# Four shared 8 KB tiles for early heads and first weights, in a clustered attention, FFN and soft-MoE kernel

## The chip, the cores and the metric

The kernel runs on one core of one Trainium2 chip. The metric is device time in microseconds (us) of one execution, lower is better. A core has five engines, each with its own instruction queue that runs in order: PE (TensorE, matrix products), DVE (VectorE), ACT (ScalarE), POOL (GpSimd) and SP (SyncE, which here only issues DMAs). An engine that comes to an instruction whose inputs are not ready waits, and everything behind it in its queue waits too.

## The reference

Three stages follow one another. In the first, 16 pairs of batch and head (2 x 8, called heads below) each have 768 tokens of 64 numbers; every query and key is put to its nearest of 16 centroids, and attention is restricted to pairs of the same cluster. The second is a feed-forward layer, and the third a soft mixture of 8 experts with 4 slots each, whose slot weights are a softmax over all 1,536 tokens and whose combine weights are a softmax over the 32 slots:

```python
q_assign = np.argmax(np.einsum('bhsd,hcd->bhsc', q_n, c_n), axis=-1)
scores = np.where(mask, scale * np.matmul(q, k.transpose(0, 1, 3, 2)), -1000000000.0)
x = softmax(scores) @ v                      # [1536, 512] after merging heads
h = x @ w_in                                 # [1536, 2048]
x = (h * np.clip(h + 3.0, 0.0, 6.0) / 6.0) @ w_out
logits = x @ phi                             # [1536, 32]
slot_input = softmax(logits, axis=0).T @ x   # [32, 512]
slot_out[e] = np.maximum(slot_input[e] @ w1[e], 0.0) @ w2[e]
out = softmax(logits, axis=1) @ slot_out     # [1536, 512]
```

## The kernel before, in words

Everything is one core's work; large products are done on fp16 pairs (a high part and the remainder). The 1,536 tokens are 12 tiles of 128, six to a batch.

**Stages.** Attention (up to about 300 us) goes head by head. For head i: `load` fetches q, k and v; `cast_hi` and `cast_lo` split q and k; a transposing DMA on SP turns them into `qk1t_i`; `as_mm` and `as_max` find each token's cluster; `as_put` writes the cluster marks beside q and k, and a second transposing DMA makes `qk2t_i`; `maxq` (products into the tile sm_i_n, L534) and `maxr` (a DVE reduction into mxs, L550) find the row maxima for the six tiles; `shift` (L557, L559) turns the maxima with PE and writes them into rows 96 to 101 of qk2t_i with DVE; only then can `scores` (L572, L576, tiles st_i_t) begin, followed by `exps`, `plow` and `pv`. Beside the heads run the preparation of the FFN weights (`win`, `wout`, `narrow` with lines L893, L895 and L897, which turns 64-bit weights into 32-bit ones) and, for tiles of the first batch, the token stage: `hid` (L726, tile h), `act` (tiles r and ghl, turned into gt either by a DMA or, for tiles 6, 7, 10 and 11, by PE into the tile gp and a copy, L763 and L768), `logits` (lg, L777), column maxima, and the slot sums `dispatch` (z, L834). The second batch's tokens follow from 300 to about 390 us. Then come slot inputs (zt, si, sit), expert layer 1 (e, L1393), layer 2 (o, L1430 and L1450), the slot outputs (so, L1336) and the combination (po, L1370) with the output DMAs.

**What sets the order.** Each function is a generator, one piece of work per `yield`, entered once as an event with `ev`. `flush` runs the pieces in the order of a long string of event numbers, ORDER. A second string, ROOMS, names for most tiles which of a tag's buffers they take. Filler products (`keep`, tile kw, L363) compute nothing that is used; there are 136 of them.

**Weights of the experts.** 36 chunks of 1 MB (four of them the product of w_out and phi's side, `wos`; sixteen of w1; sixteen of w2) are fetched by `fetch` (L1019 to L1076) into rooms: 4 in ring_a, 10 in ring_b, 1 in ring_c and others in tiles that the token stage gives up (x, w0 to w3, r, ghl, gt). Ring_b's rooms exist only once the pool of the attention tiles is closed (`close`, L1160). The last ten chunks reuse rooms that layer 1 has read:

```python
rooms = ["a"] * NRA + ["b"] * NRB + ["c"] * NRC + ["x.g", "w0", "w1", "w2", "w3", "x.r", "ghl", "gt", "ghl"]
rooms += ["a"] * 2 + ["b"] * 9 + ["c"]
```

**The end.** `slots_out(p)` and `combine(p, b)` (L1351 to L1386) run for p = 0 (384 of the 512 output columns) and p = 1 (128), and for each batch b. For p = 0 a batch has three pairs of tiles, copied out of PSUM by ACT and DVE in turn; the first two pairs share one output DMA of 768 KB (L1381), the third has one of 384 KB (L1384). Batch 0's DMAs are issued by ACT, batch 1's by SP.

Of the kernel before, what the change touches and what calls it, by code (L numbers as in the profile page):

```python
# [222 lines left out]
NRA = 4  # L223
WHOLE = ("024", "024", "024", "024", "024", "024", "024", "024", "", "", "", "", "", "", "", "")
TURNED = {6, 7, 10, 11}
NRB = 10
NRC = 1


@with_exitstack  # L230
def clustered_attention_ffn_softmoe(ctx: ExitStack, tc, q, k, v, cent, w_in, w_out, phi, w1, w2, out):
# [924 lines left out]
    for n in range(NRA):  # L1156
        evf()
# [368 lines left out]
```

## Time and profile before

| | us |
|---|---|
| median of 3 runs | 454.58 |
| the three runs | 454.5, 454.58, 462.92 |
| the profiled execution, its own time | 454.56 |
| its span, first to last instruction or DMA | 452.6 |
| mean granted clock of PE over the span | 0.989 of full |

The profile is one execution. Its times count from the span's start. The time of an execution is the span and some 2 us around it.

### The profile page before, as it was taken

Reading aid. Unit: us, or ns where it says so; the run is one execution under the profiler, and the core shown is the slowest. Engines: PE = TensorE matmul, PEld = TensorE weight load, DVE = VectorE, ACT = ScalarE, POOL = GpSimd, SP = SyncE. Lnnn points to the kernel's source line nnn. Section 1 sums busy time; section 2 is a strip of 40 time slices with the busy share of each in tenths; the row PEclk is TensorE's granted clock in tenths of the full one; section 3 lists DMA queues with packets and bytes.
Section 4 is the critical chain, followed back from the end, with each engine's and each line's share of the span. In section 5 each row is a group of like instructions: output and inputs, shape, how many; then the busy total and the mean of one; then the engine's idle time right before and its main releaser. Section 6 shows DMA issues by size and latency. Waiting matters only on the chain.

```text
span 452.6 us, 11711 instructions
## 1 busy us (share of the span) xinstructions
PE 430.9 (95%) x4866; PEld 275.6 (61%) x4866; DVE 275.5 (61%) x481; ACT 307.3 (68%) x506; POOL 251.8 (56%) x229
## 2 busy tenths in 40 slices
PE   7899999999999989999999999999999999789982
PEld 6567877787887555666656567764655455523332
DVE  5999988999877587465736768512543236621223
ACT  7799997999999868978887897974343545301011
POOL 6558695775756675797876777994133323130000
PEclk9999998999999999999999999999999999989998
DMA  7999766977596996367831876009999999999978
GB/s 268 267 240 244 185 144 197 222 215 217 211 285 105 307 191 135 111 136 138 156 100 37 276 138 94 4 2 222 240 337 313 310 232 290 326 314 353 383 195 279
DMA packets 126612, 95.23 MB, mean 210 GB/s; under 512 B 95328, under 2 KB 111712, under 8 KB 126560
## 3 DMA queue, kind: packets, MB, share of 16 engines
q1 hardware_dynamic: 122656, 88.69, 75.1%
q10 hardware_dynamic: 3904, 5.80, 3.5%
q8 instruction: 38, 0.62, 0.6%
q14 instruction: 14, 0.11, 0.1%
HBM read 64.06 MB, written 7.34 MB: 158 GB/s over the span
## 4 chain that ended last, share of the span: by engine, by line
PE 80%; DMA 7%; DVE 6%; ACT 3%; POOL 1%; issue 1%; SPq 0%; ACTq 0%; DVEq 0%
PE h L726 26%; PE acc L642 7%; PE st L572 6%; PE st L576 6%; PE sm L534 6%; DMA wk<-in_moe_w_dram 5%; PE acc L648 3%; PE acc L647 3%; PE acc L655 3%; PE z L834 2%; PE kw L363 2%; PE lg L777 2%; PE tp L966 1%; DMA qk1t<-qk 1%; DVE mxs L550 1%; PE gp L763 1%
## 5 line engine op out<-in xcount | busy, mean ns | idle before, releaser
L354 POOL TENSOR_TENSOR pp<-p,pp 128x768 f16<-128x768 f32 x72 | 119.1, 1661 | 52.4 <-ACT pp L344 25.2
L726 PE MATMUL h<-wq,xt 128*128 128x512 f16 x576 | 134.4, 379 | 0.0
L550 DVE TENSOR_REDUCE mxs<-sm 128x1 f32<-128x768 f32 x96 | 89.6, 953 | 22.9 <-PE sm L534 21.8
L726 PEld LDWEIGHTS <-xt 128*128 128x128 f16 x576 | 54.1, 97 | 58.2 <-issue 1.7
L354 POOL TENSOR_TENSOR ghl<-r,ghl 128x1024 f16<-128x1024 f32 (+1 forms) x25 | 50.3, 2015 | 56.8 <-ACT ghl L344 56.7
L620 ACT ACTIVATE p<-st 128x768 f32<-128x768 f32 x72 | 57.7, 808 | 10.8 <-PE st L576 9.2
L344 ACT ACTIVATE pp<-p 128x768 f16<-128x768 f32 x72 | 60.4, 844 | 1.7 <-PE acc L655 0.7
L572 PE MATMUL st<-qk1t 128*128 128x384 f16 x192 | 47.2, 327 | 1.4 <-DVE qk2t L559 1.2
L576 PE MATMUL st<-qk2t 102*128 102x384 f16 x192 | 47.3, 327 | 0.0
L534 PE MATMUL sm<-qk2t 80*128 80x384 f16 x192 | 45.2, 325 | 1.5 <-DVE wi L897 0.8
L743 ACT ACTIVATE r<-h,b_relu 128x1024 f32<-128x1024 f32 (+1 forms) x26 | 27.0, 1049 | 25.8 <-PE h L726 12.3
L745 DVE SCALAR_TENSOR_TENSOR r<-r,h 128x1024 f32<-128x1024 f32 (+1 forms) x26 | 29.4, 1136 | 19.5 <-ACT r L743 19.3
L344 ACT ACTIVATE ghl<-r 128x1024 f16<-128x1024 f32 (+1 forms) x26 | 25.5, 988 | 17.3 <-DVE r L745 10.6
L648 PE MATMUL acc<-v,pp 128*128 128x64 f16 x432 | 36.4, 194 | 0.0
L647 PE MATMUL acc<-v,pp 128*128 128x65 f16 x432 | 36.4, 193 | 0.0
L642 PE MATMUL acc<-v,pp 128*128 128x65 f32 x288 | 35.8, 274 | 0.3 <-DVE ohs L477 0.2
L642 PEld LDWEIGHTS acc<-v,pp 128*128 128x128 f32 x288 | 34.8, 192 | 1.9 <-DVE ohs L477 0.6
L647 PEld LDWEIGHTS <-pp 128*128 128x128 f16 x432 | 31.6, 100 | 4.0 <-issue 0.8
L354 POOL TENSOR_TENSOR qk<-qk,qk 128x768 f16<-128x768 f32 x15 | 24.7, 1646 | 12.1 <-ACT qk L344 11.1
L648 PEld LDWEIGHTS <-pp 128*128 128x128 f16 x432 | 29.5, 96 | 3.1
L344 ACT ACTIVATE qk<-qk 128x768 f32<-128x768 f32 (+2 forms) x32 | 26.3, 822 | 3.7 <-DMA qk1t<-qk 2.6
L576 PEld LDWEIGHTS <-qk2t 102*128 102x128 f16 x192 | 18.8, 98 | 13.1 <-issue 0.7
(197 smaller groups left out, 763.0 us busy)
## 6 DMA issues: line engine op xcount, KB each, us to landing
wk<-in_moe_w_dram SPq DMA_DIRECT2D x48, 512.0 KB, 5.9
wi<-in_moe_w_in_dram SPq DMA_DIRECT2D x16, 512.0 KB, 5.8
wod<-in_moe_w_out_dram SPq DMA_DIRECT2D x16, 512.0 KB, 5.3
wos<-wo ACTq DMA_DIRECT2D x8, 512.0 KB, 3.1
wk<-wos SPq DMA_DIRECT2D x8, 512.0 KB, 6.9
qk<-in_q_dram SPq DMA_DIRECT2D x16, 192.0 KB, 3.4
qk<-in_k_dram SPq DMA_DIRECT2D x16, 192.0 KB, 5.0
v<-in_v_dram SPq DMA_DIRECT2D x16, 192.0 KB, 2.9
```

The costliest lines, as they stand in the source:

```text
L344: nc.scalar.activation(out, in_, AF.Copy, scale=scale)
L354: (nc.vector if e == "v" else nc.gpsimd).tensor_tensor(out=out, in0=in_, in1=hi, op=ALU.subtract)
L534: nc.tensor.matmul(s[:, j, 0:384], d["qk2t"][0:80, n, 0], d["qk2t"][0:80, 3 * j : 3 * j + 3, 1], start=True, stop=True,)
L550: nc.vector.tensor_reduce(out=mxs[i % 2][:, 96 + n : 97 + n], in_=s[:, :, 0:384], op=ALU.max, axis=AX.XY)
L572: nc.tensor.matmul(s[:, j, 0:384], d["qk1t"][:, t, 1], d["qk1t"][:, 3 * j : 3 * j + 3, 0], start=True, stop=False)
L576: nc.tensor.matmul(s[:, j, 0:384], d["qk2t"][0 : 96 + NT, t, 1], d["qk2t"][0 : 96 + NT, 3 * j : 3 * j + 3, 0], start=False, stop=True,)
L620: nc.scalar.activation(p32, s[:, :, 0:384], AF.Exp, scale=sc_exp)
L642: nc.tensor.matmul(o, p32[:, j, r * P : (r + 1) * P], d["v32"][:, t], start=(t == 0 and n == 0), stop=False)
L647: nc.tensor.matmul(o, hi, v1[:, t, 0:65], start=(t == 0 and n == 0), stop=False)
L648: nc.tensor.matmul(o[:, 0:64], hi, v1[:, t, 65:129], start=False, stop=False)
L726: nc.tensor.matmul(s[:, fb % 2], xt[:, lhs], wq[fb][:, hl, kk], start=(n == 0), stop=(n == 11))
L745: nc.vector.scalar_tensor_tensor(out=g, in0=r, scalar=6.0 * SG, in1=sf, op0=ALU.min, op1=ALU.mult)
```

## The change

Four tiles `pr_0` to `pr_3` of 8 KB per partition are made once, beside the constants, and live through the whole kernel. `piece` cuts smaller tiles out of them. During attention they hold the two q/k load tiles and the staging copy `sp` (pr_0); the split q/k tile, the centroid tiles and narrow's scratch (pr_1); two of the three qk2 tiles, v of the even heads and the centroid pair (pr_2); qk1t and qk2t of heads 0, 4, 8 and 12 and v of the odd heads (pr_3). So v has two buffers in place of one, qk1t and qk2t have three and a shared one in place of four, and ring_b shrinks from 10 rooms to 6. The four tiles then take weight chunks 4 to 7, which no longer have to wait for the attention pool to close, and later chunks 26 to 29.

Chunk 16 goes into two tiles of turned activations (x.x) in place of x.r, and late_x moves to the tag r. The last token tile's copies of gt, all four on DVE before, go half to ACT. For p = 0 `combine` issues one DMA of 384 KB per pair of tiles. In layer 1 the events stay, and the new ORDER runs expert group 0's first two steps, group 1's first three, then group 0's last two and group 1's last. Numbering of events changes (HEADS, the interleaving of win and wout), and ORDER and ROOMS are new throughout. PE has as many instructions as before, 136 fillers included.

```diff
-    "9 0 8 12 15 0 9 16 12 12 817 15 16 1 807 7 10 835 8 838 11 816 16 16 16 16 8 825 834 8 836 4 16 8 17 20 13 0 "
...
+    "0 837 807 9 811 8 9 809 0 15 15 803 829 840 0 0 0 16 16 16 16 16 5 10 8 11 13 13 842 848 834 820 8 8 16 16 8 "
...
-NRB = 10
+NRB = 6
+NRP = 4
+LDR = "0101001011010011"
+HEADS = (0, 1, 2, 3, 4, 6, 5, 7, 8, 9, 10, 11, 12, 14, 13, 15)
...
+    pr = [cp.tile([P, 2048], F32, name=f"pr_{i}") for i in range(NRP)]
+
+    def piece(i, a, shape, dt):
+        n = 1
+        for x in shape:
+            n *= x
+        b = mybir.dt.size(dt)
+        t = pr[i].bitcast(dt)[:, a // b : a // b + n]
+        if len(shape) == 3:
+            return t.rearrange("p (a b c) -> p a b c", a=shape[0], b=shape[1])
+        return t.rearrange("p (a b) -> p a b", a=shape[0]) if len(shape) == 2 else t
...
-    qk2 = [ap.tile([P, NT, 2, P], F16, name=f"qk2_{i}", bufs=1) for i in range(NZ)]
+    qk2 = [piece(2, 3072 * i, [NT, 2, P], F16) for i in range(2)]
+    qk2.append(ap.tile([P, NT, 2, P], F16, name="qk2_2", bufs=1))
...
-            t = st[i]["v"] = ap.tile([P, NT, D], F32, tag="ldv", name=f"v_{i}", bufs=1)
+            t = st[i]["v"] = piece(2 + i % 2, 6144, [NT, D], F32)
...
-        d["qk1"] = ap.tile([P, NT, 2, P], F16, tag="qk1", name=f"qk1_{i}", bufs=1)
+        d["qk1"] = piece(1, 0, [NT, 2, P], F16)
...
+    def turned_tile(k, i):
+        if i % 4 == 0:
+            return piece(3, 3072 * (k == "qk2t"), [NT, 2, P], F16)
+        return ap.tile([P, NT, 2, P], F16, tag=k, name=f"{k}_{i}", bufs=3)
...
-        if last and f0 % 2 == 0:
+        if t == NTOK - 1 and f0 in (1, 2):
             nc.scalar.copy(d["gt"][:, f0:f1], tp)
...
-            s = raw[nm, "s"] = ap.tile([P, 1024], U32, tag="nw", name=f"nw_{nm}", bufs=1)
+            s = raw[nm, "s"] = piece(1, 4096, [1024], U32)
...
-    rooms = ["a"] * NRA + ["b"] * NRB + ["c"] * NRC + ["x.g", "w0", "w1", "w2", "w3", "x.r", "ghl", "gt", "ghl"]
-    rooms += ["a"] * 2 + ["b"] * 9 + ["c"]
+    early = [f"p{i}" for i in range(NRP)]
+    rooms = ["a"] * NRA + early + ["b"] * NRB + ["c"] * NRC + ["x.g", "x.x", "w0", "w1", "w2", "w3", "ghl", "gt", "ghl"]
+    rooms += ["a"] * 2 + early + ["b"] * (NRB - 1) + ["c"]
...
-    for n in range(NRA):
+    for n in range(NRA + NRP):
         evf()
...
-            if p == 0 and u == 1:
-                dma(out=dst[:, 0:4, c0 : c0 + w], in_=four)
+            if p == 0:
+                dma(out=dst[:, 2 * u : 2 * u + 2, c0 : c0 + w], in_=o)
                 yield
-        if p == 0:
-            dma(out=dst[:, 4:NT, c0 : c0 + w], in_=two)
-        else:
+        if p:
             dma(out=dst[:, :, c0 : c0 + w], in_=four)
```

Three places show what the new order moves. The lines of the kernel after stand some 14 to 23 higher than those of the kernel before.

The first is DVE at the end of the maxima of head 9, about 159 us. Before:

```order
L550 TENSOR_REDUCE mxs_1_114<-sm_9_3_2750 128x1
L550 TENSOR_REDUCE mxs_1_114<-sm_9_4_2777 128x1
L550 TENSOR_REDUCE mxs_1_114<-sm_9_1_2822 128x1
L550 TENSOR_REDUCE mxs_1_114<-sm_9_5_2835 128x1
L893 TENSOR_SCALAR nw_o3_0_2848<-wod_3_0_2714 128x1024
L559 SCALAR_TENSOR_TENSOR qk2t_9_2634<-sm_9_5_2835,nident_85 6x6x128
L991 SCALAR_TENSOR_TENSOR wp2_92<-wpo_2_2801,wp2_92 128x4x32
L897 SCALAR_TENSOR_TENSOR wo_3_2846<-nt_o3_0_2847,nw_o3_0_2848 128x1024
```

After, where pr_1 is narrow's scratch tile:

```order
L569 TENSOR_REDUCE mxs_1_116<-sm_9_4_2729 128x1
L569 TENSOR_REDUCE mxs_1_116<-sm_9_1_2746 128x1
L912 TENSOR_SCALAR pr_1_104<-wod_3_0_2600 128x1024
L1010 SCALAR_TENSOR_TENSOR wp2_92<-wpo_2_2738,wp2_92 128x4x32
L569 TENSOR_REDUCE mxs_1_116<-sm_9_3_2760 128x1
L569 TENSOR_REDUCE mxs_1_116<-sm_9_5_2800 128x1
L916 SCALAR_TENSOR_TENSOR wo_3_2757<-nt_o3_0_2758,pr_1_104 128x1024
L578 SCALAR_TENSOR_TENSOR qk2t_9_2577<-sm_9_5_2800,nident_85 6x6x128
```

The integer shift of `narrow` (TENSOR_SCALAR on wod_3_0) that stood between the last maximum and the writing of qk2t_9 now stands two reductions earlier; in its old place is narrow's other step, the SCALAR_TENSOR_TENSOR into wo_3.

The second is DVE at the last token tile, about 385 us. Before:

```order
L783 TENSOR_TENSOR l4_10_6461<-l_all_95,lg_10_6425 128x128
L768 COPY gt_11_6463<-gp_11_0_6464 128x1024
L354 TENSOR_TENSOR ghl_11_6365<-r_11_1_6423,ghl_11_6365 128x512
L798 TENSOR_REDUCE tm_10_6495<-lt_10_6489 128x1
L801 TENSOR_SCALAR nm_10_6497<-tm_10_6495,nm_9_6316 128x1
L768 COPY gt_11_6463<-gp_11_2_6500 128x1024
L768 COPY gt_11_6463<-gp_11_1_6476 128x1024
L768 COPY gt_11_6463<-gp_11_3_6511 128x1024
L825 TENSOR_TENSOR dhl_10_6533<-pe_10_6531,dhl_10_6533 128x32
```

After:

```order
L802 TENSOR_TENSOR l4_10_6378<-l_all_95,lg_10_6343 128x128
L368 TENSOR_TENSOR ghl_11_6281<-r_11_1_6339,ghl_11_6281 128x512
L817 TENSOR_REDUCE tm_10_6422<-lt_10_6415 128x1
L820 TENSOR_SCALAR nm_10_6424<-tm_10_6422,nm_9_6256 128x1
L787 COPY gt_11_6385<-gp_11_0_6400 128x1024
L787 COPY gt_11_6385<-gp_11_3_6433 128x1024
L844 TENSOR_TENSOR dhl_10_6453<-pe_10_6451,dhl_10_6453 128x32
```

Two of four copies of gt_11 have left DVE (ACT has them now, the second right before et_10), and the first copy has moved behind the low part of ghl_11 and behind tm_10 and nm_10.

The third is SP at the close of attention, where DMAs of wk and pr fetch expert weights, gt and xt are transposes of the token stage. Before, from the last transpose for a head to those of token tile 5 and of xt_3:

```order
L496 DMA_TRANSPOSE qk2t_15_4846<-qk2_0_104 128x12x128
L754 DMA_TRANSPOSE gt_4_5157<-ghl_4_4410 128x16x128 x2
L1075 DMA wk_4_5518<-in_moe2_w1_dram 128x1024
L1075 DMA wk_5_5524<-in_moe2_w1_dram 128x1024
L1075 DMA wk_6_5546<-in_moe2_w1_dram 128x1024
L710 DMA_TRANSPOSE xt_3_5189<-xhl_1_3010 128x8x128
L754 DMA_TRANSPOSE gt_5_5561<-ghl_5_4781 128x16x128 x2
L1075 DMA wk_7_5580<-in_moe2_w1_dram 128x1024
```

After:

```order
L1097 DMA wk_3_4726<-wos_107 128x2x512
L1097 DMA pr_0_103<-in_moe2_w1_dram 128x1024
L1097 DMA pr_1_104<-in_moe2_w1_dram 128x1024
L1097 DMA pr_2_105<-in_moe2_w1_dram 128x1024
L1097 DMA wk_0_4584<-wos_107 128x2x512
L773 DMA_TRANSPOSE gt_4_5166<-ghl_4_4317 128x16x128 x2
L1097 DMA pr_3_106<-in_moe2_w1_dram 128x1024
L1097 DMA pr_0_103<-in_moe2_w1_dram 128x1024
L1097 DMA pr_1_104<-in_moe2_w1_dram 128x1024
L773 DMA_TRANSPOSE gt_5_5490<-ghl_5_4718 128x16x128
L729 DMA_TRANSPOSE xt_3_5110<-xhl_1_2985 128x8x128
L773 DMA_TRANSPOSE gt_5_5490<-ghl_5_4718 128x16x128
```

Three halves of w1 chunks now stand ahead of gt_4, and six ahead of gt_5 and xt_3, in the shared tiles pr_0 to pr_3; in the kernel before none stood ahead of gt_4, and three, in ring_b's rooms, ahead of xt_3 and gt_5.

## Rows read from the trace of the kernel before

**Rows 1.** The page, part 1: busy us by engine, share of span, instructions.
```profile
PE 430.9 (95%) x4866; PEld 275.6 (61%) x4866; DVE 275.5 (61%) x481; ACT 307.3 (68%) x506; POOL 251.8 (56%) x229
```

**Rows 2.** Stretches: length, busy (instructions) by engine, granted clock, DMA share, GB/s.
```profile
290.00:300.00 10.00, 10.00 (x137) 6.32 (x134) 1.56 (x4) 9.12 (x12) 9.13 (x6) 1.00 0.01 2
390.00:400.00 10.00, 7.49 (x100) 4.17 (x98) 4.31 (x11) 1.74 (x7) 3.16 (x20) 1.00 0.87 281
```

**Rows 3.** Waits of PE from 60 to 380 us: us in total, times, longest.
```profile
PE st L572 <- DVE qk2t L559: 1.2, 1, 1.2
PE sm L534 <- DVE wi L897: 0.8, 1, 0.8
```

**Rows 4.** Stretches of 2 us, columns as in rows 2.
```profile
72.00:74.00 2.00, 1.82 (x20) 1.62 (x19) 1.86 (x5) 1.64 (x5) 0.31 (x1) 0.93 0.00 0
74.00:76.00 2.00, 2.00 (x34) 1.56 (x31) 1.89 (x4) 1.29 (x3) 2.00 (x2) 0.50 1.12 205
76.00:78.00 2.00, 2.00 (x14) 1.70 (x13) 1.13 (x2) 1.37 (x3) 1.94 (x2) 0.71 0.97 268
402.00:404.00 2.00, 2.00 (x16) 0.64 (x12) 0.28 (x1) 0.00 (x0) 0.00 (x0) 0.50 0.95 344
446.00:448.00 2.00, 0.00 (x0) 0.00 (x0) 0.00 (x0) 0.00 (x0) 0.00 (x0) 1.00 1.02 312
```

**Rows 5.** Timeline of DVE, 156 to 166 us: start, us, instruction.
```profile
159.08 0.96 DVE L550 TENSOR_REDUCE mxs<-sm 128x1 f32<-128x768 f32 x1 [0.67 <-PE sm L534]
159.95 2.17 DVE L893 TENSOR_SCALAR nw_o<-wod 128x1024 uint32<-128x1024 uint32 x1
162.15 0.96 DVE L559 SCALAR_TENSOR_TENSOR qk2t<-sm,nident 6x768 f16<-6x768 f32 x1
...
163.35 1.21 DVE L897 SCALAR_TENSOR_TENSOR wo<-nt_o,nw_o 128x1024 uint32<-128x1024 uint32 x1
```

**Rows 6.** Timeline of PE, 159 to 165 us.
```profile
160.46 1.46 PE L726 MATMUL h<-wq,xt 128*128 128x512 f16 x6
163.16 0.48 PE L572 MATMUL st<-qk1t 128*128 128x384 f16 x2 [1.25 <-DVE qk2t L559]
```

**Rows 7.** Timeline of DVE, 383 to 445 us.
```profile
386.75 1.88 DVE L768 COPY gt<-gp 128x1024 f16<-128x1024 f16 x3
```

**Rows 8.** Timeline of PE, 385 to 453 us.
```profile
387.49 0.38 PE L363 MATMUL kw<-ident,ident 128*128 128x256 f16 x2 [0.65 <-DVE gt L768]
...
433.63 2.12 PE L1450 MATMUL o<-wk,late_w 128*32 128x384 f32 x18 [0.58 <-DMA wk<-in_moe_w_dram]
...
438.52 1.14 PE L1370 MATMUL po<-late_a,late_a 96*128 96x384 f16 x6 [1.17 <-DVE late_a L1347]
439.58 1.08 PE L1450 MATMUL o<-wk,late_w 128*32 128x128 f32 x32
```

**Rows 9.** Timeline of ACT, 383 to 453 us.
```profile
386.87 0.37 ACT L807 ACTIVATE et<-lt,nm 128x128 f32<-128x128 f32 x1 [1.62 <-DVE nm L801]
...
440.40 0.39 ACTq L1381 DMA_DIRECT2D out_dram<-late_w  x1
...
446.41 1.13 ACTq L1384 DMA_DIRECT2D out_dram<-late_gt  x1
```

**Rows 10.** Timeline of SP's DMA issues, 300 to 453 us.
```profile
305.87 1.31 SPq L1075 DMA_DIRECT2D wk<-in_moe_w_dram  x3
...
442.42 0.38 SPq L1381 DMA_DIRECT2D out_dram<-late_w  x1
```

**Rows 11.** DMA issues: count, KB each, median us to landing.
```profile
wk<-in_moe_w_dram SPq DMA_DIRECT2D x48, 512.0 KB, 5.9
...
out_dram<-late_w ACTq DMA_DIRECT2D x1, 768.0 KB, 4.7
...
out_dram<-late_gt ACTq DMA_DIRECT2D x1, 384.0 KB, 5.2
```

**Rows 12.** Timeline of ACT, the first 27 us.
```profile
12.33 0.80 ACT L405 COPY qk2t<-tq 128x768 f16<-128x768 f16 x1 [0.50 <-PE tq L401]
```

More of the change, by code (lines that the diff above doesn't have):

```diff
@@ L368, in load @@
         if part == 0:
-            t = st[i]["qk"] = ap.tile([P, 2, NT, D], F32, tag="ld", name=f"qk_{i}", bufs=2)
+            t = st[i]["qk"] = piece(0, 3072 * int(LDR[i]), [2, NT, D], F32)
             for n, src in enumerate((q, k)):
@@ L418, in cast_lo @@
         yield
-        d["qk1t"] = ap.tile([P, NT, 2, P], F16, tag="qk1t", name=f"qk1t_{i}", bufs=4)
+        d["qk1t"] = turned_tile("qk1t", i)
         if i == 0:
@@ L491, in as_put @@
         yield
-        d["qk2t"] = ap.tile([P, NT, 2, P], F16, tag="qk2t", name=f"qk2t_{i}", bufs=4)
+        d["qk2t"] = turned_tile("qk2t", i)
         if i == 0:
@@ L848, in centroids @@
     def centroids():
-        c32 = ap.tile([P, D], F32, tag="acp", name="c32", bufs=1)
+        c32 = piece(1, 3072, [D], F32)
         nc.scalar.dma_start(out=c32, in_=cent.rearrange("h c d -> (h c) d"))
@@ L853, in centroids @@
         yield
-        sq = ap.tile([P, D], F32, tag="csq", name="csq", bufs=1)
+        sq = piece(1, 3328, [D], F32)
         ss = sm.tile([P, 1], F32, tag="tm", name="css")
@@ L865, in centroids @@
         nc.vector.reciprocal(r, y)
-        cn = ap.tile([P, D], F32, tag="cn", name="cn", bufs=1)
+        cn = piece(1, 3584, [D], F32)
         nc.vector.tensor_scalar(out=cn, in0=c32, scalar1=r, scalar2=SQ, op0=ALU.mult, op1=ALU.mult)
-        cin = ap.tile([P, 4, D], F16, tag="ms", name="cin", bufs=1)
+        cin = piece(2, 7680, [4, D], F16)
         cb = cn.unsqueeze(1).to_broadcast([P, 2, D])
@@ L977, in wphi2 @@
         yield
-        sp = ap.tile([P, 512], F32, tag="wps", name=f"wps_{j}", bufs=1)
+        sp = piece(0, 6144, [512], F32)
         nc.scalar.copy(sp, pp)
@@ L1010, in room @@
     def room(n, m, size, nm):
+        if m[0] == "p":
+            return pr[int(m[1])]
         if m in rings:
@@ L1103, in clustered_attention_ffn_softmoe @@
     ev(phs_load)
-    for i in range(NH):
+    for i in HEADS:
         if i == H:
@@ L1128, in clustered_attention_ffn_softmoe @@
         ev(keep, 7 + n, 2)
-    for n in range(8):
-        kk, hf = divmod(n, 2)
-        ev(win_load, kk, hf)
-        for part in range(5):
-            ev(win, kk, hf, part)
-    for n in range(8):
-        j, hf = divmod(n, 2)
+    for kind, j, hf in [("i", n // 2, n % 2) for n in range(6)] + [
+        (x, j, hf) for j0 in range(4) for hf in range(2) for x, j in (("o", j0),) + ((("i", 3),) if j0 == 0 else ())
+    ]:
+        if kind == "i":
+            ev(win_load, j, hf)
+            for part in range(5):
+                ev(win, j, hf, part)
+            continue
         ev(wout_load, j, hf)
@@ L1206, in lt2k @@
             elif k == "x":
-                t = mo.tile([P, 1024], F32, tag="xt", name="late_x", bufs=NT // 2)
+                t = mo.tile([P, 1024], F32, tag="r", name="late_x")
             else:
@@ L1468, in clustered_attention_ffn_softmoe @@
         ev(slot_in, c)
-        evf()
+        if c < 2:
+            evf()
     ev(slot_t)
```

340 rows, old and new, of tables (ORDER, ROOMS) are left out of this document.

## Prediction

> **What bounds the kernel now.** Read the page's first part first: PE is busy 430.9 of 452.6 us [rows 1]. So 21.7 us of idle PE are all that better order can win, apart from work done at a lower clock, and no part of the change removes products: the fillers and the instruction count stay. Then read stretches of 10 us to see where the idle time lies: the long middle is full, as the row from 290 us (10.00 of 10.00), while the row from 390 us, where the expert stage begins, has 7.49 [rows 2]. Third, the waits of PE between 60 and 380 us: the two largest are single ones, 1.2 us for qk2t and 0.8 us for a DVE write of wi [rows 3]. Last, look for half clock: two places show a granted clock of 0.50, at 74 and at 402 us [rows 4]. That is the lower level, 1.2 GHz in place of 2.4 GHz. Read the length from the rows beside it: 0.93 at 72 us is 0.3 us of half clock in 2, then 2.0, then 1.2 for 0.71, in all 3.4 us at half speed, so 1.7 us of work lost. I take the second one as equal. Before the first, PE had stood in the wait of 0.8 us.
>
> The profiled execution took 454.56 us against a median of 454.58, so its rows can carry the sum; 2.0 us of it lie outside the span.
>
> **Part by part. Head 9.** Before, DVE ends the last maximum at 160.04 (159.08 + 0.96), and behind it stands a 2.17 us integer shift of narrow, so that qk2t is only written from 162.15 to 163.11; PE, with six h products from 160.46 as its only cover, waits 1.25 us [rows 5, 6]. In the new order the shift stands two reductions earlier and the 1.21 us step into wo takes its place. Count from the end of sm_9_5 on PE: reduction 0.96, wo 1.21, done at 2.2. PE has twelve h products in that time, two groups of six at 1.3 to 1.46, so 2.6 to 2.9; the small transpose of the maxima follows, and qk2t is written 0.96 later, at about 3.9 to 4.1. Behind the transpose PE now has six products of acc, six of h and eighteen of acc ahead of st_9: 1.3 us of h and, by my estimate, 0.7 to 0.9 us of acc, which ends at about 4.8. So the write is ready first, by some 0.7 us, and the wait of 1.25 goes. Next late there is nothing within 0.7 us. The shift of 2.17 us has not vanished: it delays the two later reductions, but these have the twelve h products ahead of their use. Bounds: -1.25 if all is won, +1.0 if the moved shift makes an earlier reduction late by half its length. I take -1.2, since the margin is on the side of the wait going.
>
> **The write of wi near 71 us.** The wait of 0.8 us [rows 3] is for a PSUM tile that narrow's last step frees; the new order keeps the same step in front of the same product, with more of head 2's acc products spread around it. And the half clock at 74 us comes just behind it [rows 4]. I take 0; the bounds are -2.5 (the wait and the dip both go: 0.8 + 1.7) and +1.7 (a second dip elsewhere in the 40 us of rearranged opening heads).
>
> **The opening.** ACT's first copies are reordered, and a copy of the same size (about 0.8 us) now stands ahead of the copy of qk2t of head 0, which had waited 0.50 for PE [rows 12]: that copy starts 0.3 us later. DVE's half of the same tile comes later still and hides most of it. Bounds 0 and +0.8; I take +0.2.
>
> **Weights fetched early.** Three halves of w1 chunks go out before gt_4 and six before gt_5 and xt_3, where before three went out together at 305.87, once attention's pool was closed [rows 10]. They move into an idle stretch: DMA share 0.01 from 290 to 300 us [rows 2]. But PE is 10.00 busy there and until 380, with no wait for a weight [rows 2, 3], so the cover was complete and an earlier fetch wins nothing there. It also does not thin the traffic that PE does wait for: the ten chunks fetched into rooms that layer 1 frees are as many as before, and PE's wait of 0.58 at 433.63 is for one of them [rows 8]. What the tiles cost on the other side is room in attention, where a shared tile holds parts of several heads at once; I find no new wait behind it and leave it in the +1.7 above. On the SP queue each load is issued in well under a microsecond, 1.31 for three [rows 10]; a transpose behind a load that waits for its tile is the danger (slower rival). I take 0, bounds -1.0 (the DMA waits of layer 2: 0.58 and a smaller one before it) and +5.9, one landing of 512 KB [rows 11].
>
> **Two copies of gt for ACT.** Three copies take DVE 1.88 us from 386.75 [rows 7], and PE waits 0.65 for the first of them [rows 8]. ACT is idle 1.62 us before its et [rows 9]. A copy of 768 columns takes ACT 0.80 [rows 12], so one of 1,024 about 1.1 (estimate). With two on each, DVE's last ends about 0.6 earlier (one copy fewer behind nm), ACT's second is hidden in its 1.62. This is a chain: logits, the last maximum, et, zt and si all hang on it, so it counts. I take -0.5; bounds -0.65 and +0.4, the second if ACT's second copy pushes et back.
>
> **The tail.** PE waits 1.17 us for late_a before po, and afterwards spends 1.08 on the first half of o2_1_1 [rows 8]. The new order puts that half into the wait: about 1 us for so_1 and what hangs on it, less 0.4 because the po of batch 1 now runs against PSUM tiles not yet copied. The first output DMA is issued when the first pair is copied, some 0.5 us ahead of 440.40, and of batch 1's 768 KB at 442.42 [rows 9, 10] the first half goes up to 1 us earlier. From there the end is transfers: a DMA share of 1.02 at 446 to 448 [rows 4], and a last issue at 446.41 with 5.2 to landing, 451.6 [rows 9, 11]. DVE's last copy, late_gt, now comes at the end, so the last issue is hardly earlier (446.3, estimate); the gain is that less is still in flight then. I take -0.6; bounds -1.2 and +0.6.
>
> By the Trainium skill (DMA: Bandwidth & Descriptors, section "Anatomy of one DMA — SWDGE (gpsimd) path") a DMA costs a fixed 2 us besides its bytes; by that the two further DMAs add up to 4 us where they don't overlap, and the sum would end near 456.5, the side of the last rival below. Here 768 KB land in 4.7 us and 384 KB in 5.2 [rows 11], which agrees with a part that doesn't shrink with the bytes; but the engines are full at the same time [rows 4], so it overlaps, and I do not add it.
>
> **Layer 1's new order** changes which room comes free when: the first still after group 0's second step. With the same products, 0. The half clock at 402 us [rows 4] follows waits of the same chain as before; 0, bounds -1.7 and +1.7.
>
> Sum: -1.2 + 0.2 - 0.5 - 0.6 = -2.1 from 454.56, so 452.5 us. A measurement of this kernel can tell about 2%, 9.1 us, from no change: faster means below 445.5, slower above 463.7.
>
> **Rivals.** *Gain given back* (chance 0.22): the 1.2 us of head 9 only brings PE sooner to a wait at heads 10 to 12 whose producers (DVE, POOL) have not moved, and at the end the landing that ended the wait at 433.63 holds it. For: DVE is the releaser of both large waits [rows 3]. Against: the transfers start when layer 1 frees rooms, which moves along. Only gt's part is left, 454.1.
>
> *The dips go* (0.18): the 0.8 us wait, both half-clock stretches (2 x 1.7) and the DMA wait of 0.58 disappear together: 452.5 - 0.8 - 3.4 - 0.6 = 447.7, and somewhat below 446 if the row from 390 us gains more. For: the dips follow spells of idle PE, and the order is new at both. Against: si, sit and e wait in a chain that no part shortens.
>
> *A load blocks SP* (0.10, slower): a load into pr_3 or a second one into pr_0 waits for the last reader of a head's tile, and gt_4, gt_5 and xt_3 queue behind it. Once gt_4 lands after PE has used up the hidden products it has, PE stands for up to one landing, 5.9 [rows 11], and a stop of that kind brings half clock, 1.7: 452.5 + 7.6 = 460.1. Against: before, SP stood at its first w1 loads until 305.87 and PE did not wait at all [rows 2, 10], so there is slack of many microseconds.
>
> *Output DMAs in series* (0.05, slower): were two 384 KB transfers of a queue run one behind the other, a pair takes 2 x 5.2 in place of 4.7 [rows 11], +5.7: 458.2. Against: the full engines [rows 4].
>
> **How the numbers follow.** My forecast has 0.45, with its own range 450.5 to 454.0. Below 446.5 lies the lower part of the dips' case, some 0.06; above 458 most of the two slower ones, 0.12. So 446.5 to 458 holds about 8 in 10. Faster by over 2% needs the dips' case and 2 us more: 0.06. Slower by over 2% needs a blocked SP twice over: 0.04. Within 2%: 0.90.
>
> **What would show it.** Right: no wait of st on qk2t near 159 us in PE's waits; PE's wait for gt at the last token tile smaller by about half a microsecond; po starting without idle time behind o2_1_1; eight output DMAs that start about half a microsecond sooner; weight traffic spread into 285 to 305 us with PE unchanged. Wrong: a wait of PE for gt, xt or wk between 280 and 380 us; a third stretch at clock 0.50; the wait at 433.63 grown by what was won upstream; output traffic below a share of 1 behind 442 us.

## The result, and the profile after

The kernel after takes 449.66 us, the median of 6 runs (448.08 to 451.0), against 454.54 before: a ratio of 0.9914, 95% interval 0.9884 to 0.9943. By that ratio it is 3.9 us faster (2.6 to 5.3), and within 2%; the two medians lie 4.9 apart. The forecast was 452.5, in a range of 446.5 to 458. The profiled execution took 451.0, its span is 449.1. The same kernel, run again beside the last experiments, gave 448.89 (0.9888, 0.9842 to 0.9934). The profiles of two of the runs below, a and g, are of slow executions (460.72 and 459.0 us), with a half clock from 33 us on, so only what lies behind 90 us is read from them.

Read the page's first part and the same stretches as in [rows 1, 2, 4], columns as there:

```profile
PE 429.5 (96%) x4866; PEld 276.1 (61%) x4866; DVE 274.9 (61%) x479; ACT 309.8 (69%) x508; POOL 251.1 (56%) x229
```

```profile
290.00:300.00 10.00, 10.00 (x160) 6.96 (x158) 1.42 (x4) 8.99 (x12) 8.86 (x6) 1.00 0.22 81
390.00:400.00 10.00, 7.65 (x101) 4.30 (x104) 2.88 (x8) 0.57 (x3) 4.06 (x26) 1.00 0.97 366
...
74.00:76.00 2.00, 2.00 (x31) 1.79 (x30) 1.97 (x4) 2.00 (x4) 1.05 (x2) 1.00 1.27 155
...
400.00:402.00 2.00, 2.00 (x16) 0.58 (x12) 1.28 (x4) 0.52 (x1) 0.00 (x0) 0.50 1.02 414
```

PE's busy time is 1.4 us less with the same instructions: the half clock at 74 us is not there, that near 400 us is. From 390 us on the DMA share is 0.97 where it had been 0.87.

The waits of PE between 60 and 378 us, to be laid beside [rows 3]:

```profile
PE st L591 <- DVE r L764: 0.6, 1, 0.6
PE st L591 <- DVE wo L916: 0.5, 1, 0.5
PE tp L985 <- DVE mxs L569: 0.5, 1, 0.5
PE sm L553 <- ACT wot L989: 0.2, 1, 0.2
PE st L591 <- DVE mxs L569: 0.2, 1, 0.2
```

The wait of 1.2 for qk2t and that of 0.8 for wi are gone, and five small ones have come, with two more at 50 us (0.65 and 0.18).

Where the 3.5 us between the two profiled spans went is read from PE's timeline, as the start of the same work in each. The last column is worked out from the one before it.

| start on PE, us | before | after | moved since the row above |
|---|---|---|---|
| first scores that use qk2t (st) | 25.23 | 25.51 | +0.28 |
| logits of the last but one tile (lg) | 382.83 | 381.44 | -1.67 |
| slot sums turned (zt) | 391.71 | 390.36 | +0.04 |
| layer 1 (e) | 400.82 | 399.61 | +0.14 |
| slot outputs (so) | 435.68 | 432.64 | -1.83 |
| combination (po) | 438.52 | 435.48 | 0.00 |
| end of the span | 452.6 | 449.1 | -0.46 |

So the attention and token stages gave 1.67, about what one stretch of half clock costs; the gt copies gave nothing; the expert layers gave 1.83, where the forecast had nothing; the tail gave 0.46. The expert layers' part shows in SP's timeline. Before, the first loads into rooms that layer 1 frees:

```profile
406.19 0.81 SPq L1075 DMA_DIRECT2D wk<-in_moe_w_dram  x2
```

After, the same loads and the next two, and PE's one wait for such a load, which answers to 433.63 in [rows 8]:

```profile
402.94 0.81 SPq L1097 DMA_DIRECT2D pr<-in_moe_w_dram  x2
404.99 0.93 SPq L1075 DMA_DIRECT2D pr<-in_moe_w_dram  x2
```

```profile
430.59 2.12 PE L1471 MATMUL o<-wk,late_w 128*32 128x384 f32 x18 [0.76 <-DMA wk<-in_moe_w_dram]
...
435.48 1.14 PE L1393 MATMUL po<-late_a,late_a 96*128 96x384 f16 x6 [0.15 <-DVE late_a L1370]
```

From the first of these issues to the end of PE's last wait are 27.4 us before (406.19 to 433.63) and 27.7 after (402.94 to 430.59). In these two profiles the loads last as long as before; they start 3.25 us earlier. Of that, 1.2 comes from layer 1's own earlier start (e in the table), and 2.0 from something that the prediction missed.

### The profile page after: what moved, and what is told of

The parts are those of the page before. It is cut to its first block, busy times and chain, and to the rows that moved or that the text cites. A ratio compares the mean times of both kernels' runs of the same rounds, so it can differ in the third digit from the quotient of the medians.

```text
span 449.1 us, 11732 instructions
## 1 busy us (share of the span) xinstructions
PE 429.5 (96%) x4866; PEld 276.1 (61%) x4866; DVE 274.9 (61%) x479; ACT 309.8 (69%) x508; POOL 251.1 (56%) x229
## 4 chain that ended last, share of the span: by engine, by line
PE 73%; DVE 11%; DMA 6%; ACT 5%; issue 2%; POOL 1%; SPq 0%; DVEq 0%; ACTq 0%; POOLq 0%
PE h L745 27%; PE st L591 5%; PE sm L553 5%; PE st L595 5%; DVE mxs L569 4%; PE acc L661 4%; PE acc L674 3%; DMA wk<-in_moe_w_dram 2%; PE acc L667 2%; PE acc L666 2%; DMA pr<-in_moe_w_dram 2%; PE z L853 2%; PE kw L377 2%; PE lg L796 2%; DMA qk1t<-pr 1%
## 5 line engine op out<-in xcount | busy, mean ns | idle before, releaser
L591 PE MATMUL st<-qk1t 128*128 128x384 f16 x144 | 35.1, 325 | 2.3 <-DVE qk2t L578 0.7
L595 PE MATMUL st<-qk2t 102*128 102x384 f16 x144 | 35.2, 325 | 0.0
L553 PE MATMUL sm<-qk2t 80*128 80x384 f16 x144 | 34.4, 325 | 0.7 <-ACT wot L989 0.2
L368 POOL TENSOR_TENSOR pr<-pr,pr 128x768 f16<-128x768 f32 x15 | 25.2, 1677 | 13.6 <-ACT pr L358 10.3
L358 ACT ACTIVATE pr<-pr 128x768 f32<-128x768 f32 (+2 forms) x32 | 26.3, 823 | 4.0 <-DMA qk1t<-pr 2.2
L377 PE MATMUL kw<-ident,ident 128*128 128x256 f16 x136 | 22.9, 294 | 2.6 <-POOL b_relu L870 1.7
```

Source lines behind the costliest of these rows:

```text
L358: nc.scalar.activation(out, in_, AF.Copy, scale=scale)
L368: (nc.vector if e == "v" else nc.gpsimd).tensor_tensor(out=out, in0=in_, in1=hi, op=ALU.subtract)
L377: nc.tensor.matmul(t[:, 0, 0:256], ident16, ident.bitcast(F16), start=True, stop=True)
L553: nc.tensor.matmul(s[:, j, 0:384], d["qk2t"][0:80, n, 0], d["qk2t"][0:80, 3 * j : 3 * j + 3, 1], start=True, stop=True,)
L591: nc.tensor.matmul(s[:, j, 0:384], d["qk1t"][:, t, 1], d["qk1t"][:, 3 * j : 3 * j + 3, 0], start=True, stop=False)
L595: nc.tensor.matmul(s[:, j, 0:384], d["qk2t"][0 : 96 + NT, t, 1], d["qk2t"][0 : 96 + NT, 3 * j : 3 * j + 3, 0], start=False, stop=True,)
```

## The experiments

Twelve kernels ran. Two theories on the expert layers were set against each other. S: from about 388 us on the stream of weights bounds the end, and it starts again sooner. A room is a buffer of 1 MB that takes a chunk in two halves; a persistent tile is released half by half, where a newly allocated one waits for all readers of the tile before it. P: PE's own order at the start of layer 2 made the gain. Event numbers in ORDER are those of the kernel that is changed. The table collects what the readings below rest on: the time is the median, the ratio that of the run beside the kernel before, and all other columns come from one profile, in us; "none" means that no half clock (0.50) stood ahead of 440 us.

| run | time, ratio to before | half clock near | zt | first load into a freed room | so | zt to so | po to end |
|---|---|---|---|---|---|---|---|
| before | 454.54 | 74, 402 us | 391.71 | 406.19 | 435.68 | 43.97 | 14.08 |
| before again | 454.66, 0.9995 | 402 | 391.17 | 405.64 | 434.56 | 43.39 | 14.11 |
| after | 449.66, 0.9914 | 400 | 390.36 | 402.94 | 432.64 | 42.28 | 13.62 |
| after again | 448.89, 0.9888 | none | 389.44 | 400.62 | 430.03 | 40.59 | 13.64 |
| a: before, half a room | 452.08, 0.9955 | 33 to 49 | 399.19 | 410.25 | 441.17 | 41.98 | 14.60 |
| b: after, whole room | 449.88, 0.9925 | none | 389.45 | 402.35 | 431.26 | 41.81 | 13.71 |
| c: after, old start of layer 2 | 449.54, 0.9891 | none | 389.02 | 400.20 | 429.35 | 40.33 | 13.72 |
| d: after, gt on DVE | 449.82, 0.9906 | 400 | 391.25 | 403.84 | 432.55 | 41.30 | 13.92 |
| e: after, 768 KB outputs | 450.13, 0.9906 | 400 | 390.16 | 402.61 | 431.85 | 41.69 | 14.01 |
| f: after, shift of narrow back | 452.09, 0.9962 | 400 | 392.33 | 404.16 | 433.59 | 41.26 | 13.68 |
| g: before, shift of narrow earlier | 453.99, 0.9978 | 33 to 47, 81 to 84 | 397.37 | 410.15 | 440.05 | 42.68 | 14.22 |
| h: after, late loads ahead of gt_5 | 456.44, 1.0069 | 316 to 322 | 396.08 | 407.27 | 437.38 | 41.30 | 13.69 |
| h2: after, late loads behind gt_5 | 449.33, 0.9894 | none | 390.21 | 401.39 | 430.85 | 40.64 | 13.72 |
| i: after, old order of layer 1 | 451.23, 0.9944 | 400 | 389.35 | 401.85 | 434.22 | 44.87 | 13.55 |

**The two kernels again.** Nothing is changed in either.

> The kernel before, unchanged, for a second profile. If the half-clock stretches fall where they like, the one at 74 us (1.7 us lost) is absent or elsewhere, and from the first scores to the logits of tile 10 it takes, without them, about 355.9 us, as the kernel after. If the one at 74 us belongs to the old order, it is there again, and the stretch takes 357.6. A run of the same kernel beside itself: a ratio of 1 within its interval.

> The kernel after, unchanged, as the yardstick for the runs beside it: about 449.7. The two half-clock stretches of the kernel before (at 74 and 402 us) and the one of after (about 400 us) were seen in one profile each; in two variants of after none stood ahead of 440 us. If they fall where they like, this profile has another set of them than the first one of the same kernel, and its stretch from the first scores to the logits of tile 10 is, without them, again 355.9 us.

Columns as in rows 2. Before again, at 74 us:

```profile
74.00:76.00 2.00, 2.00 (x41) 1.81 (x41) 2.00 (x4) 2.00 (x5) 1.42 (x1) 1.00 0.60 111
```

After again, at 400 us:

```profile
400.00:402.00 2.00, 2.00 (x24) 0.65 (x20) 1.52 (x5) 0.31 (x1) 0.00 (x0) 1.00 1.02 412
```

Each lost one stretch that its first profile had, with the same instructions. Before again still waited 0.8 for wi and 1.24 for qk2t. From the first st to lg of the last but one tile it took 356.17 us; the kernel after took 355.93 and 355.95. So nearly all of the 1.67 that the first two profiles show for attention is the half clock at 74 us, and the new order of attention is worth 0.2.

**a and b, the release of half a room.** In a, chunks 26 and 27 are written into the tiles of chunks 5 and 6 themselves:

```diff
         if m in rings:
-            return rings[m].tile([P, size], F32, tag="w", name=nm)
+            if n in (26, 27):
+                return kept[n - 21]
+            t = rings[m].tile([P, size], F32, tag="w", name=nm)
+            if n in (5, 6):
+                kept[n] = t
+            return t
```

> The kernel before with one thing changed: chunks 26 and 27 are written into the very tiles of chunks 5 and 6 instead of newly allocated ones in the same rooms, so their first halves wait only for the readers of those halves (layer 1's first step) and no longer for the whole tile. Theory S (from about 388 us on the weight stream bounds the end, and it starts again sooner because half a room comes free sooner): SP's first issue into such a room moves from 406.2 to about 404.0, the start of so_0 from 435.7 to about 434.0, the time by -1.0 to -2.0 us, to about 453. Rival P (the end of layer 2 is set by PE's own order of ht and fillers): the issue moves, so_0 and the time don't, 454.5.

In b, the half that layer 1's second step reads is asked for first:

```diff
-        for c in range(2):
+        for c in (1, 0) if n in (26, 27) else (0, 1):
```

> The kernel after, with the two halves of chunks 26 and 27 fetched in the opposite order, so that the first to be issued waits for layer 1's second step. Theory S: first issue from 402.9 to about 405.0, PE's wait for wk in layer 2 grows by 1 to 2 us, so_0 from 432.6 to about 434.2, the time +1.0 to +2.0, about 451.2. Rival P: so_0 and the time unchanged, 449.7.

b and the kernel after again are the same to 0.01 us up to zt. Then SP's first load, of after again first and of b second:

```profile
400.62 0.81 SPq L1097 DMA_DIRECT2D pr<-in_moe_w_dram  x2
```

```profile
402.35 0.81 SPq L1097 DMA_DIRECT2D pr<-in_moe_w_dram  x2
```

and the wait that they end, in the same order:

```profile
427.98 2.12 PE L1471 MATMUL o<-wk,late_w 128*32 128x384 f32 x18 [0.91 <-DMA wk<-in_moe_w_dram]
```

```profile
429.21 2.12 PE L1471 MATMUL o<-wk,late_w 128*32 128x384 f32 x18 [0.77 <-DMA wk<-in_moe_w_dram]
```

The start 1.73 us later gives 1.23 at PE's wait and 1.23 at so. The order of PE is the same, so P can't explain it. The times alone don't show it: b's ratio of 0.9925 (0.9895 to 0.9956) overlaps both of the kernel after, and the time was expected at about 451.2, where 449.88 was measured. In a the time fell by 2.0 us (0.9955, 0.9923 to 0.9987), with one thing changed. Its profile shows the first load 1.95 us behind e, against 3.67 in g, which has the old release and, as a, full clock there. SP's timelines, a first, g second:

```profile
410.25 0.86 SPq L1081 DMA_DIRECT2D wk<-in_moe_w_dram  x2
```

```profile
410.15 0.80 SPq L1076 DMA_DIRECT2D wk<-in_moe_w_dram  x2
411.05 0.38 SPq L1054 DMA_DIRECT2D wk<-in_moe_w_dram  x1
```

But zt to so is only 0.7 shorter than in g, so most of the 2.0 in a's time is not explained by its profile.

**c, the old start of layer 2.**

```diff
-1159 1159 1160 1147 ... 1166 1166 1146 1153 1153 1162 1148 ... 1161 1163 1167 ... 1142 1167 ...
+1159 1159 805 1160 1147 ... 1166 1166 1146 1153 1153 1161 1127 1167 1167 1128 1120 1162 1148 ... 1163 ... 1142 ...
```

(1161 and 1167 are the turns of h1, 1162 is layer 2, 805, 1127, 1128 and 1120 are fillers, eight products in all, which the kernel after runs behind po.)

> The kernel after, with the order of layer 2's start as in the kernel before: the second transpose of group 1 and four more fillers (8 products) ahead of o2_0. Theory S: o2_0 starts about 1.7 us later, but PE's wait for wk (0.76) shrinks or goes, and so_0 and the time move by 0 to +0.9. Rival P: so_0 and the time +1.7 to +2.1, about 451.6.

PE's timeline, after again first, then c:

```profile
414.20 3.64 PE L1451 MATMUL o<-wk,late_w 128*32 128x512 f32 x32
...
430.03 1.67 PE L1359 MATMUL so<-late_w,late_a 128*96 128x384 f32 x4
```

```profile
416.19 3.64 PE L1451 MATMUL o<-wk,late_w 128*32 128x512 f32 x32
...
429.35 1.67 PE L1359 MATMUL so<-late_w,late_a 128*96 128x384 f32 x4
```

Counted from zt, layer 2 starts 2.4 us later in c and so 0.3 earlier; the wait of 0.91 is gone. Part of the 2.4 is work that only moved ahead, but the eight filler products are added ahead of so, and so is no later for them. P falls: its 1.7 to 2.1 us are not there.

**i, the old order of layer 1.**

```diff
-1144 1145 1143 1155 1156 1143 1116 1117 1157 1150 1151 1142
+1144 1145 1150 1151 1143 1155 1156 1143 1116 1117 1157 1142
```

(1144, 1145, 1150 and 1151 are group 0's steps, 1155 to 1157 group 1's.)

> The kernel after, with layer 1 in the order of the kernel before: group 0's four steps, then group 1's, everything else left. The first rooms still come free at the same time. Theory S with rooms: the next load in SP's order waits for a room that group 1's second step frees, and that now comes 3.4 us later, so SP stands, the weight stream has a gap, and so_0 comes 1.5 to 3.5 us later: 450.5 to 452.5. Rival (the order of layer 1 is indifferent, as the prediction had it): so_0 within 0.4 us, 449.2.

SP's timeline and PE's waits for loads:

```profile
401.85 0.80 SPq L1097 DMA_DIRECT2D pr<-in_moe_w_dram  x2
403.98 0.93 SPq L1075 DMA_DIRECT2D pr<-in_moe_w_dram  x2
410.86 0.37 SPq L1075 DMA_DIRECT2D wk<-in_moe_w_dram  x1
```

```profile
PE o L1471 <- DMA wk<-in_moe_w_dram: 2.9, 2, 2.1
```

and the stretch in which the engines run dry, columns as in rows 2:

```profile
410.00:412.00 2.00, 2.00 (x24) 0.61 (x20) 0.69 (x1) 0.60 (x1) 0.00 (x0) 1.00 0.48 150
```

SP stands for 5.9 us between its second and third load, DMA falls to 150 GB/s (384 in the kernel after), and zt to so is 2.6 us longer than in the first profile of after, which has the same half clock. The order of layer 1 is not indifferent. But i keeps the new rooms, in which chunk 30 takes the room of chunk 13, one that group 1's second step frees; its zt to so of 44.87 is longer even than in the kernel before. So 2.6 is the price of an order that doesn't fit the rooms, and not a comparison with the old order in its own rooms.

**h and h2, the loads of chunks 4 to 7 late.** In h six of the loads (events 1026 to 1029) stand right behind the close of the pool:

```diff
-1007 1030 1049 1051 ... 1040 1018 1018 1041 1031
+1007 1030 1026 1027 1028 1026 1027 1029 1049 1051 ... 1040 1018 1018 1041 1031
```

> The kernel after, with the loads of chunks 4 to 7 issued only once the attention pool is closed, as before. Theory of the prediction and theory S alike: nothing waits for them before layer 1, so the time stays within 0.5 us of the unchanged kernel after. Rival E (the early 4 MB thin the traffic that the end waits for): the weight stream from 388 us on starts or ends later, time +1 or more.

In h2 they stand four transposes further on:

```diff
-1040 1018 1018 1041 1031
+1040 1018 1018 1041 1026 1027 1028 1029 1026 1027 1031
```

> The kernel after, with the loads of chunks 4 to 7 moved behind the close of the pool and behind the transposes of gt_5, xt_3 and xt_4, so that no transpose that is soon needed stands behind them. Theory of the prediction: nothing waits for them before layer 1, time within 0.6 us of the kernel after (449 to 450). Rival E (the early 4 MB themselves matter): the weight stream from 388 us on starts or ends 1 us later or more, or PE waits for xt_5, time 451 or more.

SP's timeline and PE's waits from 300 to 330 us in h, and the clock behind the wait:

```profile
303.76 3.58 SPq L1097 DMA_DIRECT2D pr<-in_moe_w_dram  x6
307.44 4.98 SPq L729 DMA_TRANSPOSE xt<-xhl  x1
312.52 4.08 SPq L773 DMA_TRANSPOSE gt<-ghl  x1
```

```profile
PE lg L796 <- DMA gt<-ghl: 5.1, 1, 5.1
```

```profile
316.00:318.00 2.00, 0.00 (x0) 0.00 (x0) 0.00 (x0) 0.00 (x0) 0.00 (x0) 0.50 1.28 289
```

In h2 the second transpose of gt_5 goes out at 308.80, and the six loads only at 316.69. h2 is as fast as the kernel after (0.9894); h is 7.5 us slower than it. The six early loads, 3 MB, are worth nothing in themselves: the prediction's 0 stands. The same six ahead of two transposes, xt_3 and the second one of gt_5, cost 5.1 us of wait, with a half clock that began in it; both theories had said nothing of that, and the expectation missed it.

**d, all copies of gt on DVE.**

```diff
-        if t == NTOK - 1 and f0 in (1, 2):
-            nc.scalar.copy(d["gt"][:, f0:f1], tp)
-        else:
+        if True:
             nc.vector.tensor_copy(d["gt"][:, f0:f1], tp)
```

> The kernel after, with all four copies of the last token tile's gt on DVE. Theory of the prediction (DVE's copies set the logits of the last tile): lg of that tile and all behind it 0.5 us later, 450.2. Rival G (POOL's low part of ghl, for which PE now waits 0.63, is what comes last): the logits move by less than 0.2 us, the time stays at 449.7.

PE's timeline of d:

```profile
384.57 0.40 PE L782 MATMUL gp<-ident,ghl 128*128 128x128 f16 x4 [0.63 <-POOL ghl L368]
...
388.00 0.20 PE L794 MATMUL lg<-wp,gt 128*128 128x64 f16 x1 [0.84 <-DVE gt L785]
```

The logits start at 386.58, as in the kernel after (386.52), but stand inside for a copy, and zt comes 0.9 later from lg on. At so nothing is left of that (432.55 and 432.64), and the times can't be told apart. The stream of weights doesn't explain it simply: d's first load into a freed room comes 0.9 later too (403.84 against 402.94), and yet PE's last wait for a load ends at 430.50 against 430.59. SP and PE in d:

```profile
403.84 0.80 SPq L1095 DMA_DIRECT2D pr<-in_moe_w_dram  x2
```

```profile
430.50 2.12 PE L1469 MATMUL o<-wk,late_w 128*32 128x384 f32 x18 [0.22 <-DMA wk<-in_moe_w_dram]
```

So the start of the stream alone doesn't set its end, and what made up the 0.9 us is not shown. Neither theory had it whole.

**e, the output DMAs as before.**

```diff
-            if p == 0:
-                dma(out=dst[:, 2 * u : 2 * u + 2, c0 : c0 + w], in_=o)
+            if p == 0 and u == 1:
+                dma(out=dst[:, 0:4, c0 : c0 + w], in_=four)
+            elif p == 0 and u == 2:
+                dma(out=dst[:, 4:NT, c0 : c0 + w], in_=two)
```

> The kernel after, with combine's output DMAs as before: one of 768 KB for the first two pairs of tiles. Theory of the prediction: from po to the end +0.6 us (bounds -0.6 and +1.2), 450.3. Rival (the fixed part of a DMA counts when it is split): the end comes earlier by 0.5 us or more.

From po to the end e takes 14.01 us, the kernel after 13.62 and 13.64. That is 0.4 in the direction of the forecast, but d, with the split, took 13.92, so a single profile shows it barely; the times of the two can't be told apart.

**f and g, head 9.** In f, narrow's shift (927) goes back between the last maximum (480) and the writing of qk2t (481):

```diff
-472 942 927 475 515 ... 943 927 480 930 945 929 608 607 481 444 481 608
+472 942 475 515 ... 943 480 927 930 945 608 607 481 444 481 927 929 608
```

> The kernel after, with narrow's integer shift of wod_3_0 back between the last maximum of head 9 and the writing of qk2t_9 (and its two next steps behind it). Theory of the prediction: PE waits about 1.2 us for qk2t there, and the logits of tile 10 and all behind come 1.2 us later. Rival (given back): PE waits there, but later waits shrink, and the logits of tile 10 move by less than 0.4 us.

In g, it goes two reductions forward in the kernel before:

```diff
-471 478 942 466 472 479 480 446 444 927 946
+471 478 927 942 466 472 479 480 446 444 946
```

> The kernel before, with narrow's integer shift of wod_3_0 moved ahead of the last two reductions of head 9 and nothing else. Theory of the prediction: PE's wait of 1.25 us for qk2t of head 9 goes, and the logits of tile 10 come 1.0 to 1.25 us earlier, time 453.5. Rival (given back): the wait goes, but the next one in the old order grows, and the logits of tile 10 move by less than 0.4 us.

PE's timeline in f, and DVE's in g, to be laid beside [rows 5]:

```profile
164.82 1.46 PE L745 MATMUL h<-wq,xt 128*128 128x512 f16 x6 [2.13 <-DVE wo L916]
```

```profile
166.14 0.96 DVE L551 TENSOR_REDUCE mxs<-sm 128x1 f32<-128x768 f32 x1 [0.67 <-PE sm L535]
167.72 0.96 DVE L560 SCALAR_TENSOR_TENSOR qk2t<-sm,nident 6x768 f16<-6x768 f32 x1 [0.63 <-PE sm L558]
```

In f PE does not wait for qk2t, but h waits 2.13 for the PSUM tile that the delayed step into wo frees; the stretch from st to lg is 2.3 us longer (358.24), so all of it is kept to the end of attention, and the time is 3.2 us above that of the kernel after again. In g the writing of qk2t starts 1.58 us behind the start of the last reduction (167.72 less 166.14), against 3.07 before, and PE no longer waits for it. PE's timeline, before first, then g:

```profile
160.35 0.27 PE L557 MATMUL sm<-ident,mxs 128*102 128x128 f32 x1
...
177.30 0.96 PE L966 MATMUL tp<-ident,wo 128*128 128x128 f32 x7 [0.42 <-DVE r L745]
```

```profile
167.41 0.27 PE L558 MATMUL sm<-ident,mxs 128*102 128x128 f32 x1
...
182.96 1.06 PE L967 MATMUL tp<-ident,wo 128*128 128x128 f32 x8 [0.42 <-DVE r L746]
```

From that transpose of the maxima to the wait at tp PE took 16.95 us before (160.35 to 177.30) and takes 15.55 in g (167.41 to 182.96), 1.4 less; from tp to zt both take 214.41. So in these profiles the gain is real and is not given back later in that order. Its time, 0.9978 (0.994 to 1.0017), agrees with 1.0 us but can't tell it from none.

## Why the prediction was right, and where it was not

The sign and the range were right, and -2.1 against a measured -3.9 (-5.3 to -2.6) is half of it. But that is in good part luck: head 9, the largest term, and the gt copies together brought about 0.2 in the new order, and the largest gain lies where the prediction put 0.

- **Head 9 (-1.2 forecast).** The step itself was right: in the kernel after, the last reduction begins at 160.16, wo at 161.22, qk2t at 162.86, and st at 164.69 without a wait. g shows 1.4 for it alone. The sentence that next late there is nothing held there, but the new order has seven small waits elsewhere in attention, 2.74 us in all against 2.88 before. Like for like in clock, attention moved by 0.2. The rival "gain given back" had the size, but not the place; it looked at heads 10 to 12 and at the landing at 433.63.
- **The write of wi and the half clock at 74 us (0 forecast).** The wait of 0.8, which was to stay, is gone in the kernel after. The half clock was priced rightly, 1.7, but it is not a part of the old order: before again runs without it, with the same wait of 0.8.
- **The opening (+0.2 forecast).** Between the first two profiles it is +0.28. But the first scores start between 25.02 and 26.11 in four profiles with the old opening and between 24.28 and 25.52 in ten with the new one, on average 0.5 sooner, so the sign is not borne out.
- **gt on ACT (-0.5 forecast).** ACT's copies took 1.00 us each, where the estimate was 1.1. From lg to zt nothing was won (3.90 before, 3.84 after), and PE now waits 0.63 for POOL's low part of ghl one step earlier, where it had waited 0.65 for gt. Undoing the split in the new order costs 0.9 at zt, and nothing that the profile shows at so.
- **Early loads (0 forecast).** Right, by h2. The slower rival's mechanism is real too: h comes to the same, with transposes kept behind loads, priced at 7.6 and measured at 7.5, though its wait was 5.1 where 5.9 had been put. The "slack of many microseconds" that the prediction set against it was less than that; the change itself keeps its loads clear of it.
- **Layer 1's order and the freed rooms (0 forecast).** This is the step that failed: "the first still after group 0's second step". The first room's half comes free after the first step, 1.7 us sooner (b, 402.35 against 400.62), and the new order of layer 1 frees the further rooms in the order in which the new chunks need them (i, 2.6 us without). In profiles at full clock there, zt to so takes 42.68 us with neither (g), 41.98 with the early half alone (a), 41.81 with the new order and rooms alone (b) and 40.59 and 40.64 with both (after again, h2). That speaks for both being needed, but h, which has both, took 41.30, so steps of 0.7 are no more than such a stretch varies. The prediction saw the ten chunks and the wait at 433.63, and didn't ask what starts their stream. With a half clock near 400 us alike, zt to so is 2.1 us shorter: 43.97 and 43.39 before and 42.28, 41.30, 41.69 and 41.26 in four kernels after (after, d, e, f), means of 43.7 and 41.6.
- **The tail (-0.6 forecast).** It measured -0.46, and e puts 0.4 of it to the split output DMAs, with the reserve above. The half of o2_1_1 does go into the shadow (the wait for late_a is 0.15), but po starts no sooner: 2.84 us behind so in both. The Trainium skill's fixed 2 us per DMA ("DMA: Bandwidth & Descriptors", section "Anatomy of one DMA — SWDGE (gpsimd) path") is a figure for DMAs that POOL (GpSimd) issues, while ACT and SP issue these. It does not add up here: with two more DMAs the end comes 0.4 earlier and not 4 us later, with the engines at a share of 1.0 at 444 us.

What stays open: how much of the 3.9 us beyond some 2.8 (0.2, 2.1 and 0.5) is the opening and how much is half clock, which no run held fixed. An estimate from the spans and mean granted clocks of the executions on record points to the clock. The product of the two, which takes the half clock out of a span, is 447.8 us over 108 executions of the kernel before and 444.9 over 12 of the kernel after, 2.9 apart. It is good to about 1 us, because it also takes out half clock behind PE's last work, where it costs nothing. Why the stretch of half clock near 400 us stands in five of the profiles of the new order and its variants and is absent from others was not tried.

## What to carry to other kernels

When loads into reused buffers are the last thing waited for, ask what starts them: a buffer kept as one tile and overwritten by region can take its next load as soon as a part has been read, and the order of the readers decides whether the next room is ready when SP comes to it. Where PE waits for such a stream near the end, work beside it can change without effect on the time: eight more products on PE ahead of so in c, a chain 0.9 us later in d. Before a profile's difference is put down to an order, take a second profile of the same kernel.

## What was not expected of the hardware

The granted clock fell to 0.50 at different places in executions of the same program: at 74 and 402 us and at 402 alone in the kernel before, at 400 and nowhere ahead of 440 in the kernel after. Such stretches differ in length: that in a's profile lasted 16 us, from 33 to 49 us. The mean granted clock of an execution was below 0.983 in 29 of 132 with the old opening (before, a, g) and in none of 95 with the new one; why is not shown. Layer 1 shows the price with nothing else changed: from the first e to ht the kernel after took 15.79 us with it and 14.10 without, 1.7 us.
